# A five-place ring for streamed weight factors, paid for with one buffer less for factors on their way out

## The chip, the cores and the metric

The kernel runs on one core of a Trainium2 chip. A core has a matrix engine (PE; its weight loads are shown apart as PEld), a vector engine (DVE), a scalar engine (ACT), a general-purpose engine (POOL), a queue processor that here issues nearly all transfers (SP), and 16 DMA engines. The metric is the device time of one execution in microseconds (us), as the median over runs. Before the change it is 1222.57 us over 3 runs (1222.3 to 1227.66).

## The reference

Linear attention with softmax-like features feeds a gated two-layer product. The sizes are 8 batches, 8 heads, 576 tokens of 64 dimensions, 128 features; then 4608 tokens, 512 model columns and 1536 hidden columns, all in 32 bits.

```python
def phi(x):
    proj = einsum('bhsd,df->bhsf', x, w_phi)
    proj = proj - max(abs(proj), axis=-1, keepdims=True)
    return concatenate([exp(proj), exp(-proj)], axis=-1)
q_p, k_p = phi(q), phi(k)
kv = einsum('bhsf,bhsd->bhfd', k_p, v)
z = sum(k_p, axis=2)
attn = einsum('bhsf,bhfd->bhsd', q_p, kv) / (einsum('bhsf,bhf->bhs', q_p, z)[..., None] + 1e-06)
x = attn.transpose(0, 2, 1, 3).reshape(4608, 512)
out = (x @ w_a) * (x @ w_b) @ w_out
```

## The kernel before

Every matrix product of the second half is made of three products of split values: a 32-bit number is kept as a high part and a low part (a cast on ACT, then a subtraction on DVE; the helper `split`, L153 and L160), and PE multiplies high by high, high by low and low by high.

**First pass.** Hidden columns 0 to 767 (six slices of 128) are worked on while attention still runs, in 12 blocks of 384 tokens (`moe_block`). A block makes `pa` and `pb` for each slice (L616), multiplies the two (a copy on ACT, L620, and a product on DVE, L621), splits the result into `hh` and `hl`, and at its end makes four output accumulators `po` (L639), which are copied out (L651) to a DRAM tensor `part`. The output products of a block need `hh` and `hl` of all its slices. The last four blocks, numbers 8 to 11, run after attention has ended.

**Second pass.** Hidden columns 768 to 1535 are worked on in six blocks j = 0 to 5 of 768 tokens, with a scheme of seven products of half-size factors instead of eight (`winograd`). The weights are grouped in three quads q = 0, 1, 2, each with seven factors named w11, w12, s2, s1, s3, w22, s4. I write (q, k) for one of them. One product takes the factor of w_a and the factor of w_b, 12 matmuls in all (L729); the output products (L840) take factors of w_out.

**Where the factors live.** `load_factors` makes the factors during blocks 8 to 11: raw weights come in by DMA, ACT and DVE decode them, and each factor is split into a tile of 128 x 2 x 256 values (256 KB). Those of w_a and w_b leave for DRAM (L541, tensors `kept_...`); the first three pairs also stay in tiles `first0` to `first2`. The tile of a factor that leaves has tag `kept` with five buffers (L538): a sixth factor must wait until the store of the first has landed. ACT makes the cast, so it is ACT that waits.

The 21 factors of w_out all stay, two to a tile, in the places of w_a and w_b that the first pass has done with (`home(f, nm)`, 12 places). 21 is odd: the eleventh tile is half empty. One of the 12 places is left, and after the first pass its six places of w_out come free too: seven places of 512 KB. Four become the ring (`RING`, L55), three hold parts of the output that are read back.

**The ring.** A pair of factors is fetched (`fetch`, L565, 512 KB, called `back_...`) into a place of the ring when the product that used the place is done. `feed` is called behind each product of `winograd`, and it fetches the pair that the ring needs next in that place. So with four places the pair for product n is asked for when product n-4 has ended. All fetches, loads of x for the next block (L669), read-backs of `part` (L818) and stores of the output (L825) stand in one queue on SP, which issues them in order and stops at the first that may not go yet.

**What sets the order.** The kernel is written as nested generators, but the order of instructions on each engine is set by a scheduler that simulates the program when it is built (`schedule_with_timeline_sim=True`). In the second pass's block j = 0 the products are held to the written order (`in_turn`); in blocks 1 to 5 the scheduler may put a product ahead of others. It sees the buffers and their waits, so a change of a buffer's number moves instructions elsewhere.

Of the kernel before, what the change touches and what calls it, by code (L numbers as in the profile page):

```python
# [11 lines left out]
F32R = mybir.dt.float32r  # L12
# [6 lines left out]
P = 128  # L19
# [32 lines left out]

SLICES0 = 6
T1, T2 = 384, 768
RING, FIRST = 4, 3  # L55

FACTORS, AHEAD = ("w11", "w12", "s2", "s1", "s3", "w22", "s4"), 3.2
BLOCKS_LAST = 4
# [3 lines left out]
def tile_kernel(ctx, tc, qP, qD, km, kr, vm, vr, w_phi, w_two, eye, w_a, w_b, w_out, out):  # L62
# [14 lines left out]
    B, H, _, S = qD.shape  # L77
# [79 lines left out]
    def split(hi, lo, src, eng_hi, eng_lo):  # L157

        copy(eng_hi, hi, src)
        eng_lo.tensor_tensor(lo, src, hi, op=ALU.subtract)  # L160
# [294 lines left out]
    def decode(raw, u, stage):  # L455

        low, high = raw[:, :, 0], raw[:, :, 1]
        w = stage("w", [P, 2 * DM], F32, f"w_{u}")
        g, s = w[:, :DM], w[:, DM:]
        gb, sb = g.bitcast(U32), s.bitcast(U32)
        nc.scalar.activation(g, high.bitcast(F32), AF.Prelu, scale=2.0**-112, alpha=2.0**32)
        nc.vector.tensor_scalar(sb, gb, 3, None, op0=ALU.logical_shift_left)  # L470
        yield
        nc.vector.tensor_scalar(gb, sb, 0xFF800000, None, op0=ALU.bitwise_and)
        yield
        nc.vector.scalar_tensor_tensor(g, low, 2.0**-52, g, op0=ALU.mult, op1=ALU.mult)
        return s, g

    def load_raw(p, f, nm, stage):

        cols = (sum(NFS[:p]) + f) * P
        src = {"a": w_a, "b": w_b, "o": w_out}[nm]  # L480
        raw = stage("raw", [P, DM, 2], U32, f"raw_{p}_{f}_{nm}")
        if nm == "o":
            nc.sync.dma_start(raw.rearrange("p n w -> p (n w)"), src[cols : cols + P, :].bitcast(U32))
        else:
            nc.sync.dma_start(
                raw.rearrange("p (c n) w -> p c (n w)", c=NCC),
                src.bitcast(U32)[:, 2 * cols : 2 * (cols + P)].rearrange("(c p) n -> p c n", p=P),
            )
        return raw
# [14 lines left out]
    def load_factors(q, nm, stage, places, pool):  # L504

        w32 = stage("w32", [P, 2, DM], F32, f"w32_q{q}_{nm}")
        w = [w32[:, i] for i in range(2)]
        for i in range(2):
            u = f"q{q}_{nm}_{i}"
            s, g = yield from decode(load_raw(1, 2 * q + i, nm, stage), u, stage)  # L510
            nc.vector.tensor_tensor(w[i], s, g, op=ALU.add)
            yield
        n = DM // 2
        (w11, w12), (w21, w22) = ((t[:, :n], t[:, n:]) for t in w)
        if nm == "o":
            w12, w21 = w21, w12
        sums = stage("ws", [P, 4, n], F32, f"ws_q{q}_{nm}")
        s1, s2, s3, s4 = (sums[:, i] for i in range(4))
        nc.vector.tensor_tensor(s1, w21, w22, op=ALU.add)
        nc.vector.tensor_tensor(s3, w11, w21, op=ALU.subtract)  # L520
        nc.vector.tensor_tensor(s2, s1, w11, op=ALU.subtract)
        nc.vector.tensor_tensor(s4, w12, s2, op=ALU.subtract)
        factors = dict(w11=w11, w12=w12, s2=s2, s1=s1, s3=s3, w22=w22, s4=s4)
        yield
        for k, w32 in factors.items():
            key, i = two[q, nm, k]
            shape = [P, 2, 2, n]
            name = "_".join(map(str, key))
            if key not in begun:
                begun.add(key)  # L530
                if nm != "o":
                    kept[key] = dpool.tile(shape, F32, name=f"kept_{name}")
                if key in places:
                    weights[key] = places[key][0].tile(shape, F32R, tag=places[key][1], name=f"own_{name}")
            if key in places:
                t = weights[key][:, i]
            else:
                t = pool.tile([P, 2, n], F32R, tag="kept", bufs=5, name=f"wf_q{q}_{nm}_{k}")  # L538
            split(t[:, 0], t[:, 1], w32, nc.scalar, nc.vector)
            if nm != "o":  # L540
                nc.sync.dma_start(kept[key][:, i], t.bitcast(F32))  # L541
            if k in ("w12", "s1", "w22"):
                yield
        yield
# [13 lines left out]
    def stage_second(xin, pool):  # L558

        tags = {"raw": (pool, "raw"), "w": (pool, "w"), "w32": (xin, "x32"), "ws": (pool, "w")}  # L560
        return lambda kind, shape, dt, name: tags[kind][0].tile(shape, dt, tag=tags[kind][1], bufs=2, name=name)
# [355 lines left out]
    def run(work, steps=None):  # L917

        while work and steps != 0:
            if next(work[0], work) is work:  # L920
                work.popleft()
            elif steps is not None:
                steps -= 1
# [8 lines left out]
    def home(f, nm):  # L932
        return wpool, f"w_{f}_{nm}"

    kept, begun, feeds = {}, set(), []
# [28 lines left out]
    xin = ctx.enter_context(tc.tile_pool(name="xin", bufs=1))  # L964
    first_stack = ExitStack()
    first = first_stack.enter_context(tc.tile_pool(name="first", bufs=1))
    pairs = {(q, k): [(q, nm, k) for nm in "ab"] for q in range(nq) for k in FACTORS}
    outs = [(q, "o", k) for q in range(nq) for k in FACTORS]
# [7 lines left out]
    own = {key: (first, f"first{i}") for i, key in enumerate(order[:FIRST])}  # L976
    xs = [{} for _ in range(NCC // 2)]
    with ExitStack() as c:
        pool = c.enter_context(tc.tile_pool(name="stage", bufs=1))
        stage = stage_second(xin, pool)  # L980
        ahead = itertools.chain(
            *(load_factors(q, nm, stage, own, pool) for q in range(nq) for nm in "ab"),
            factors_of_x(0, xin, xs),
        )
        last = work.pop()
        due = 0.0
        while work:
            run(work, 1)
            due += AHEAD
            while due >= 1:  # L990
                next(ahead, None)
                due -= 1
        for _ in ahead:
            pass
        next(last)
        outs = deque(pair for pair in pairs if pair[0] == "o")
        places = deque()
        for f in range(NFS[0]):
            next(last)
            for nm in "ab":  # L1000
                if outs:
                    own[outs.popleft()] = home(f, nm)
                else:
                    places.append(home(f, nm))
            if f % 2:
                for _ in load_factors(f // 2, "o", stage, own, pool):
                    pass
# [15 lines left out]
    while len(ring) < RING:  # L1023
        ring.append(places.popleft())
        key = order.popleft()
# [64 lines left out]
```

## Time and profile before

| what | value |
|---|---|
| median of 3 runs | 1222.57 us |
| the profiled execution | 1223.55 us |
| its span, first to last instruction | 1221.8 us |
| PE busy | 1188.0 us (97%) |
| DVE busy | 969.6 us (79%) |
| ACT busy | 779.1 us (64%) |
| granted TensorE clock, mean | 0.997 |

The profiled execution is 0.98 us above the median, and 1.75 us of it lie outside the span. Its profile cuts the span by engine, by group of instructions and by the chain of waits that ended last. The first pass's lone blocks take 691 to 809 us of the span, the second pass 809 to 1222 us, about 68 us for each of its six blocks.

### The profile page before, as it was taken

The numbers are of one execution on the slowest core, as the hardware profiler recorded it, in microseconds if no ns is written. First come the engines' busy times: TensorE is split into PE (matmuls) and PEld (weight loads), VectorE is DVE, ScalarE is ACT, GpSimd is POOL, SyncE is SP. The second block draws the span as 40 slices with busy tenths as digits, with TensorE's granted clock in tenths as the row PEclk, the third lists the DMA queues.
The fourth block names the chain that finished last, engine by engine and source line by source line (L and its number), as shares of the span: only waits on it lengthen the run. The fifth ranks groups of instructions, "written<-read, shape, count | busy, mean of one in ns | idle before, by whom it ended". The sixth has DMA issues, their size and how long they took to land.

```text
span 1221.8 us, 20189 instructions
## 1 busy us (share of the span) xinstructions
PE 1188.0 (97%) x7086; PEld 1132.8 (93%) x7086; DVE 969.6 (79%) x1733; ACT 779.1 (64%) x1656; POOL 153.2 (13%) x68
## 2 busy tenths in 40 slices
PE   8889999999999999999999999999999999999998
PEld 5567789999999999999999999999999999999997
DVE  6866888988998989898888378978768695868665
ACT  5777778878878878888788445644435352535332
POOL 2322222211222121121122000000000000000000
PEclk9999999999999999999999999999999999999999
DMA  8766764554455454545342578758586777768582
GB/s 235 220 212 178 189 187 121 152 157 123 142 144 151 132 151 118 154 135 166 108 131 55 161 242 292 255 163 315 173 272 203 233 237 225 245 202 288 171 252 82
DMA packets 146165, 225.13 MB, mean 184 GB/s; under 512 B 40912, under 2 KB 87760, under 8 KB 146064
## 3 DMA queue, kind: packets, MB, share of 16 engines
q1 hardware_dynamic: 145616, 223.58, 59.9%
q8 instruction: 56, 0.92, 0.3%
q14 instruction: 45, 0.37, 0.1%
q10 hardware_dynamic: 448, 0.26, 0.1%
HBM read 174.74 MB, written 49.05 MB: 183 GB/s over the span
## 4 chain that ended last, share of the span: by engine, by line
PE 77%; DMA 11%; DVE 7%; ACT 2%; issue 2%; SPq 1%; DVEq 0%; ACTq 0%
PE pa L616 11%; PE pb L616 11%; PE po L639 11%; PE po L840 9%; PE pa L729 9%; PE pb L729 8%; PE kvps L301 7%; PE pn L383 6%; PE pq L359 2%; DMA back_w<-kept_w 2%; PE pk L244 2%; DMA x<-xnorm 2%; DMA raw_a<-in_w_a 1%; DMA raw_o<-in_w_out 1%; DMA rec<-r 1%
## 5 line engine op out<-in xcount | busy, mean ns | idle before, releaser
L363 POOL PARTITION_ALL_REDUCE mb<-p x64 | 153.0, 2391 | 526.4 <-ACT p L360 416.8
L616 PE MATMUL pa<-xh,w_a 128*128 128x384 f32 x576 | 168.1, 344 | 3.9 <-ACT xh L153 2.2
L616 PE MATMUL pb<-xh,w_b 128*128 128x384 f32 x576 | 163.2, 341 | 0.0
L639 PE MATMUL po<-hh,w_o 128*128 128x384 f32 x576 | 154.4, 340 | 1.1 <-ACT o L651 0.7
L616 PEld LDWEIGHTS pa<-xh,w_a 128*128 128x128 f32 x576 | 106.0, 188 | 5.6 <-ACT xh L153 2.4
L639 PEld LDWEIGHTS po<-hh,w_o 128*128 128x128 f32 x576 | 104.7, 188 | 2.1 <-ACT o L651 1.0
L616 PEld LDWEIGHTS pb<-xh,w_b 128*128 128x128 f32 x576 | 105.5, 188 | 0.5
L616 PE MATMUL pa<-xl,w_a 128*128 128x384 f32 x288 | 98.4, 342 | 0.0
L639 PE MATMUL po<-hl,w_o 128*128 128x384 f32 x288 | 97.4, 340 | 0.6 <-DVE hl L160 0.6
L616 PE MATMUL pb<-xl,w_b 128*128 128x384 f32 x288 | 97.5, 338 | 0.0
L160 DVE TENSOR_TENSOR qel<-qe,qeh 128x1152 fp32r<-128x1152 f32 x46 | 62.3, 1354 | 31.2 <-ACT qeh L153 29.5
L840 PE MATMUL po<-hh_s,own_o 128*128 128x384 f32 x288 | 80.3, 336 | 0.6 <-DVE o L822 0.3
L165 DVE TENSOR_TENSOR qs<-q,qs 64x576 fp32r<-64x576 f32 x52 | 63.2, 1216 | 14.3 <-ACT qs L153 12.1
L384 ACT COPY xn<-pn 65x288 f32<-65x288 f32 x128 | 49.0, 394 | 17.0 <-PE pn L383 14.8
L840 PE MATMUL po<-hh_w,own_o 128*128 128x384 f32 x216 | 59.1, 334 | 0.0
L639 PEld LDWEIGHTS po<-hl,w_o 128*128 128x128 f32 x288 | 54.0, 188 | 1.2 <-DVE hl L160 1.2
L153 ACT CAST qeh<-qe 128x1152 fp32r<-128x1152 f32 x46 | 53.3, 1160 | 2.1 <-PE pn L383 2.0
L258 ACT ACTIVATE ke<-kd 128x512 f32<-128x512 f32 x64 | 40.8, 637 | 21.4 <-DVE kd L250 20.3
L616 PEld LDWEIGHTS pa<-xl,w_a 128*128 128x128 f32 x288 | 54.1, 188 | 0.3
L616 PEld LDWEIGHTS pb<-xl,w_b 128*128 128x128 f32 x288 | 54.1, 188 | 0.1
L367 ACT ACTIVATE qe<-p 128x576 f32<-128x576 f32 x64 | 44.5, 696 | 15.1 <-DVE qel L160 10.1
L840 PEld LDWEIGHTS po<-hh_s,own_o 128*128 128x128 f32 x288 | 52.6, 188 | 1.6 <-DVE o L822 0.6
(301 smaller groups left out, 3419.5 us busy)
## 6 DMA issues: line engine op xcount, KB each, us to landing
back_s<-kept_s SPq DMA_DIRECT2D x71, 512.0 KB
back_w<-kept_w SPq DMA_DIRECT2D x52, 512.0 KB
q<-in_qD SPq DMA_DIRECT2D x52, 288.0 KB
k<-in_km SPq DMA_DIRECT2D x55, 256.0 KB
xun<-xn SPq DMA_DIRECT2D x64, 144.0 KB
x<-xun SPq DMA_DIRECT2D x32, 288.0 KB
rb<-rec SPq DMA_DIRECT2D x32, 288.0 KB
xnorm<-x SPq DMA_DIRECT2D x32, 288.0 KB
```

What stands on the lines that cost most here:

```text
L153: eng.copy(dst, src)
L160: eng_lo.tensor_tensor(lo, src, hi, op=ALU.subtract)
L165: eng_lo.tensor_tensor(hi_lo[D:], src[D:], hi_lo[D:], op=ALU.subtract)
L301: nc.tensor.matmul(st["kv_ps", b, pr][:width, j], v_[:, j, :width], e_[:, j], start=(left == NFULL and j == 0 and n_ == 0), stop=(left == ...
L363: nc.gpsimd.partition_all_reduce(mb, p32, P, bass_isa.ReduceOp.absmax)
L367: nc.scalar.activation(e[:, 0], p32, AF.Exp)
L383: nc.tensor.matmul(pn[: D + 1, :HALF], kv_[:, 2 * j + s, :], e_[:, s, tok], **at)
L384: nc.scalar.copy(xn[: D + 1, tok], pn[: D + 1, :HALF])
L616: nc.tensor.matmul(acc, w[:, cc * P : (cc + 1) * P], x, start=(k == 0), stop=(k == 3 * NCC - 1))
L639: nc.tensor.matmul(accs[cc], w[:, cc * P : (cc + 1) * P], h, **at)
L729: in_turn(lambda: nc.tensor.matmul(acc[to][i], w_, x_, skip_group_check=True, **at), u.startswith("1_0"))
L840: in_turn(lambda: nc.tensor.matmul(acc[m, to], w_, h_, skip_group_check=True, **f), False)
```

## The change

- The ring has five places for four.
- When one pair of w_out is left (the single factor (2, s4)), it gets a tile of its own in the pool `xin`, and the place that it would have half filled is left for the ring. The shape of a tile follows the number of factors that share it.
- Tag `kept` has four buffers for five. A buffer is 128 x 2 x 256 values, as large as the new tile.

The whole diff:

```diff
-RING, FIRST = 4, 3
+RING, FIRST = 5, 3
...
             key, i = two[q, nm, k]
-            shape = [P, 2, 2, n]
+            shape = [P, len(pairs[key]), 2, n]
             name = "_".join(map(str, key))
...
             else:
-                t = pool.tile([P, 2, n], F32R, tag="kept", bufs=5, name=f"wf_q{q}_{nm}_{k}")
+                t = pool.tile([P, 2, n], F32R, tag="kept", bufs=4, name=f"wf_q{q}_{nm}_{k}")
             split(t[:, 0], t[:, 1], w32, nc.scalar, nc.vector)
...
             for nm in "ab":
+                if len(outs) == 1:
+                    own[outs.popleft()] = xin, "single"
                 if outs:
                     own[outs.popleft()] = home(f, nm)
                 else:
```

The scheduler answers with another order from block 10 of the first pass on. Two places matter below.

**PE, second pass, block j = 2.** One row of each product is shown, the first matmul of its w_a half; the number behind `back_` counts the fetched pairs, then come quad and factor. Before:

```order
L729 MATMUL pa0_1_2_2_12050<-xw11h_1_2_0_11477,back_51_2_w11_11948 128x384
...
L729 MATMUL pa0_1_2_1_11888<-xs3h_1_2_0_11660,back_50_1_s3_11934 128x384
...
L729 MATMUL pa1_1_2_2_12066<-xw12h_1_2_0_11509,back_52_2_w12_11994 128x384
...
L729 MATMUL pa0_1_2_1_11888<-xw22h_1_2_0_11664,back_53_1_w22_12010 128x384
...
L729 MATMUL pa0_1_2_2_12050<-xs2h_1_2_0_11641,back_55_2_s2_12064 128x384
...
L729 MATMUL pa2_1_2_1_11996<-xs4h_1_2_0_11733,back_54_1_s4_12035 128x384
...
L729 MATMUL pa2_1_2_2_12163<-xs1h_1_2_0_11645,back_56_2_s1_12080 128x384
```

The same stretch after the change:

```order
L729 MATMUL pa0_1_2_2_12052<-xw11h_1_2_0_11479,back_50_2_w11_11936 128x384
...
L729 MATMUL pa1_1_2_2_12068<-xw12h_1_2_0_11511,back_51_2_w12_11950 128x384
...
L729 MATMUL pa2_1_2_2_12165<-xs1h_1_2_0_11647,back_55_2_s1_12066 128x384
...
L729 MATMUL pa0_1_2_1_11890<-xw22h_1_2_0_11666,back_52_1_w22_11996 128x384
...
L729 MATMUL pa2_1_2_1_11998<-xs4h_1_2_0_11735,back_53_1_s4_12012 128x384
...
L729 MATMUL pa0_1_2_2_12052<-xs2h_1_2_0_11643,back_54_2_s2_12037 128x384
```

Product (1, s3), whose row is not shown in the second fence, now stands between (2, w12) and (2, s1). Before, (2, w11) stood ahead of (1, s3) and its written place is behind it; now (2, s1) stands ahead of three products that are written before it.

**SP, the same block.** `x32` are loads of x for the next block, with 576 and 192 columns. Before:

```order
L565 DMA back_51_2_w11_11948<-kept_2_w11_9366 128x1024
L669 DMA x32_1_3_0_11980<-xnorm4_94 128x2x576
L565 DMA back_52_2_w12_11994<-kept_2_w12_9371 128x1024
L565 DMA back_53_1_w22_12010<-kept_1_w22_9080 128x1024
L669 DMA x32_1_3_0_11980<-xnorm5_95 128x2x192
L565 DMA back_55_2_s2_12064<-kept_2_s2_9376 128x1024
```

After:

```order
L565 DMA back_50_2_w11_11936<-kept_2_w11_9366 128x1024
L565 DMA back_51_2_w12_11950<-kept_2_w12_9371 128x1024
L669 DMA x32_1_3_0_11982<-xnorm4_94 128x2x576
L565 DMA back_52_1_w22_11996<-kept_1_w22_9080 128x1024
L565 DMA back_53_1_s4_12012<-kept_1_s4_9085 128x1024
L669 DMA x32_1_3_0_11982<-xnorm5_95 128x2x192
L565 DMA back_55_2_s1_12066<-kept_2_s1_9381 128x1024
```

One more fetch stands ahead of each load of x, and (2, s1) is fetched ahead of (2, s2).

**ACT, first pass, block 10.** `wf_q1_b_s4` is the cast of factor (1, s4) of w_b; `h32_0_10_4` and `hh_0_10_4` belong to slice 4 of block 10. Before:

```order
L153 CAST wf_q1_b_s4_9241<-ws_q1_b_9173 128x256
L469 ACTIVATE w_q2_a_1_9289<-raw_1_5_a_9287 128x512
L620 COPY h32_0_10_4_9795<-pa_0_10_4_9769 128x384
L153 CAST hh_0_10_3_9757<-h32_0_10_3_9754 128x384
L153 CAST wf_q2_a_w11_9367<-w32_q2_a_9278 128x256
L153 CAST wf_q2_a_w12_9372<-w32_q2_a_9278 128x256
L153 CAST hh_0_10_4_9798<-h32_0_10_4_9795 128x384
```

After:

```order
L153 CAST hh_0_10_3_9757<-h32_0_10_3_9754 128x384
L153 CAST wf_q1_b_s4_9241<-ws_q1_b_9173 128x256
L620 COPY h32_0_10_4_9795<-pa_0_10_4_9769 128x384
L469 ACTIVATE w_q2_a_1_9289<-raw_1_5_a_9287 128x512
L153 CAST wf_q2_a_w11_9367<-w32_q2_a_9278 128x256
L153 CAST wf_q2_a_w12_9372<-w32_q2_a_9278 128x256
L153 CAST hh_0_10_4_9798<-h32_0_10_4_9795 128x384
```

The cast of slice 3 has moved ahead of factor (1, s4), and the copy of slice 4 still stands behind it.

## Rows read from the trace of the kernel before

**Rows 1.** The page of the profile: span, the busiest engine, and the chain that ended last, by engine (shares of the span).

```profile
span 1221.8 us, 20189 instructions
PE 1188.0 (97%) x7086; PEld 1132.8 (93%) x7086; DVE 969.6 (79%) x1733; ACT 779.1 (64%) x1656; POOL 153.2 (13%) x68
PE 77%; DMA 11%; DVE 7%; ACT 2%; issue 2%; SPq 1%; DVEq 0%; ACTq 0%
```

**Rows 2.** Stretches of the span (us from its start): length, then busy time and number of instructions of PE, PEld, DVE, ACT, POOL, then the granted clock, the DMA engines' busy share and GB/s. The third to the fifth are parts of the second pass's blocks 1 and 2.

```profile
200.00:700.00 500.00, 497.75 (x3309) 492.48 (x3307) 425.81 (x643) 409.60 (x842) 103.03 (x42) 1.00 0.47 135
700.00:809.00 109.00, 107.75 (x607) 106.85 (x606) 95.68 (x227) 60.64 (x143) 0.00 (x0) 1.00 0.74 250
893.00:917.00 24.00, 23.15 (x132) 22.55 (x131) 17.70 (x37) 10.11 (x23) 0.00 (x0) 1.00 0.88 295
917.00:961.00 44.00, 43.38 (x249) 42.74 (x248) 31.77 (x64) 18.32 (x41) 0.00 (x0) 1.00 0.63 199
961.00:985.00 24.00, 22.30 (x129) 22.01 (x128) 18.33 (x38) 9.85 (x22) 0.00 (x0) 1.00 0.89 295
```

**Rows 3.** What PE waited for from 840 us to the end: total us, times, longest.

```profile
PE pa L729 <- DMA back_w<-kept_w: 5.2, 4, 1.8
PE pa L729 <- ACT low L737: 0.9, 2, 0.5
...
PE pa L729 <- DMA back_s<-kept_s: 0.4, 1, 0.4
```

**Rows 4.** PE in order of time, matmuls that had to wait (start, length, then in brackets the idle time before them and what ended it).

```profile
924.21 0.44 PE L729 MATMUL pa<-xw22h,back_w 128*128 128x384 f32 x1 [0.46 <-ACT low L737]
969.86 0.41 PE L729 MATMUL pa<-xw11h,back_w 128*128 128x384 f32 x1 [1.70 <-DMA back_w<-kept_w]
1037.43 0.41 PE L729 MATMUL pa<-xw11h,back_w 128*128 128x384 f32 x1 [1.81 <-DMA back_w<-kept_w]
1128.31 0.44 PE L729 MATMUL pa<-xw22h,back_w 128*128 128x384 f32 x1 [0.46 <-ACT low L737]
1172.47 0.41 PE L729 MATMUL pa<-xw11h,back_w 128*128 128x384 f32 x1 [0.19 <-ACT top L737]
```

**Rows 5.** The chain that ended last, in order of time (start, length, what): the fetches and a load of x that stand on the chain, and two runs of 12 matmuls, as many as one product has.

```profile
895.91 4.85 DMA back_w<-kept_w
964.03 5.69 DMA back_w<-kept_w
1031.49 5.81 DMA back_w<-kept_w
1041.86 6.51 DMA back_s<-kept_s
1099.73 4.85 DMA back_w<-kept_w
1111.75 7.15 DMA x<-xnorm
1174.79 2.08 PE pa L729 x12
1176.87 2.08 PE pb L729 x12
```

**Rows 6.** SP in order of time in block 2 and, last, in block 5 (start, length, what it issues, and how many together).

```profile
964.03 0.32 SPq L565 DMA_DIRECT2D back_w<-kept_w  x1
964.44 0.39 SPq L669 DMA_DIRECT2D x<-xnorm  x1
966.11 2.40 SPq L565 DMA_DIRECT2D back_w<-kept_w  x2
...
1168.15 4.49 SPq L565 DMA_DIRECT2D back_w<-kept_w  x3
```

**Rows 7.** The chain that ended last, first pass, end of block 10.

```profile
752.05 4.54 DMA kept_s<-wf_q_b_s
...
756.95 0.42 ACT wf_q_a_w L153
...
757.73 0.55 DVE h L621
```

**Rows 8.** ACT in order of time in the same stretch.

```profile
751.32 0.41 ACT L153 CAST wf_q_b_s<-ws_q_b 128x256 fp32r<-128x256 f32 x1 [0.15 <-DMA kept_w<-wf_q_b_w]
753.52 0.68 ACT L469 ACTIVATE w_q_a<-raw_a 128x512 f32<-128x512 f32 x1 [1.79 <-DVE w_q_a L511]
754.10 0.46 ACT L620 COPY h<-pa 128x384 f32<-128x384 f32 x1
756.95 0.76 ACT L153 CAST wf_q_a_w<-w_q_a 128x256 fp32r<-128x256 f32 x2 [1.97 <-DMA kept_s<-wf_q_b_s]
758.31 0.51 ACT L153 CAST hh<-h 128x384 fp32r<-128x384 f32 x1 [0.60 <-DVE h L621]
```

**Rows 9.** DVE there, one step of the decoding of a weight, and PE there, two matmuls that had to wait.

```profile
754.70 0.43 DVE L472 TENSOR_SCALAR w_q_a<-w_q_a 128x512 uint32<-128x512 uint32 x1
...
758.88 0.44 PE L639 MATMUL po<-hh,w_o 128*128 128x384 f32 x1 [0.42 <-ACT hh L153]
759.73 0.44 PE L639 MATMUL po<-hl,w_o 128*128 128x384 f32 x1 [0.41 <-DVE hl L160]
```

## Prediction

> **What bounds the kernel now.** I read the page first: PE is busy for 97% of the span and carries 77% of the chain that ended last; DMA has 11% of it and DVE 7% [rows 1]. Then the stretches: the granted clock is 1.00 in all of them, so PE runs at the higher of its levels (2.4 GHz), and the change leaves the number of matmuls as it is. PE misses 0.85 us in 893 to 917 us and 1.70 us in 961 to 985 us, both in the last third of a block, and only 0.62 us in the 44 us between [rows 2]. So a gain can come only from gaps in PE, and these are few. The view of PE's waits over the second pass names them: 5.2 us in four waits, the longest 1.8 us, for fetched factors of kind w, 0.4 us once for one of kind s, and 0.9 us for `low`, a copy that ACT makes [rows 3]. 5.6 us is all that a deeper ring can win by itself.
>
> PE in order of time gives the place: 1.70 us at 969.86 and 1.81 us at 1037.43, each at the first matmul of (2, w11) [rows 4]. The other two share 5.2 - 1.70 - 1.81 = 1.7 us, 0.85 us each; one of them is the 0.85 us that PE misses in block 1 [rows 2]. The chain says why. A fetch for (2, w11) took 4.85, 5.69, 5.81 and 4.85 us in blocks 1 to 4 [rows 5]. PE needs it two products after it was asked for, and a product of 12 matmuls takes 2.08 us [rows 5], so 4.16 us. In block 2: 964.03 + 5.69 = 969.72, and PE starts 0.14 us later [rows 4, 5]. SP issues a load of x 0.4 us behind that fetch [rows 6], and the two share the DMA engines, which are 88 to 89% busy here against 63% between [rows 2]. Block 5 has no next block to load x for: the fetch is issued at 1168.15, and PE starts (2, w11) at 1172.47 after 0.19 us of waiting for `top`, a copy of ACT [rows 4, 6]. There the fetch took at most 4.3 us.
>
> **A, what the fifth place removes.** The fetch for a product goes out when the product five before it has ended. (2, w11) then has three products, 6.24 us, between issue and use, and (2, w12) as many. The longest of these fetches, 5.81 us, and the 0.14 us behind it make 5.95 us, so both are hidden. The wait for (1, s4), whose fetch took 6.51 us in block 3 [rows 5] and which is the 0.43 us of kind s [rows 3], has in its new place at least four products. A = -(0.85 + 1.70 + 1.81 + 0.85 + 0.43) = -5.64 us.
>
> **B, what takes its place.** The scheduler has used the room to draw another product forward: (2, s1) now stands ahead of (1, w22), (1, s4) and (2, s2). Its pair is number 55 in block 2, and 55 - 5 = 50 is (2, w11). Between the end of (2, w11) and the start of (2, s1) only (2, w12) and (1, s3) are left, again two products, 4.16 us. That is the slack which was too short for (2, w11). It is so in blocks 2, 3 and 5; in blocks 1 and 4 half of (1, w22) also stands between, which makes 4.16 + 1.04 = 5.20 us. The landing of this fetch is not in the trace, so I bound it by the five fetches of rows 5: 4.85 at the short end, 6.51 at the long one, 5.54 us on the mean. With 0.14 us behind the landing, the wait is 5.54 + 0.14 - 4.16 = 1.52 us in blocks 2 and 3 and 0.48 us in 1 and 4. Block 5 has no load of x: 4.3 + 0.14 - 4.16 gives at most 0.28 us, and I take 0.1. B = 2 x 1.52 + 2 x 0.48 + 0.1 = +4.1 us. At the short end 2 x 0.83 = +1.7; at the long end 2 x 2.49 + 2 x 1.45 + 0.28 = +8.2. I take the mean, because one more load of x, of 192 columns, stands on SP just ahead of this fetch, as one stood just behind the other. Behind the waiting matmul PE holds (1, w22) and (1, s4), whose factors are there, so the loss is not made up.
>
> The Trainium skill ("Perfetto Trace Analysis", section Identifying Performance Opportunities) says that the same gap repeating on the engine which should be saturated can mean too few buffers for the next tile. By it the cure is complete: the term would be A alone. That is the first rival below. The trace has the gap at one product, in the four blocks that load x; it agrees on the cause and does not decide whether the gap only moves.
>
> **C, the copy `low`.** PE waits 0.46 us for it at (2, w22) in two blocks [rows 4]. After the change (2, w22) stands right behind (2, s3) in four blocks. At worst all four wait, 4 x 0.46 - 0.9 = +0.9; at best nothing changes. I take +0.5.
>
> **D, four buffers for kept factors.** With five, the cast of w11 of w_a in quad 2 waits for the store of (1, s2) of w_b: 752.05 + 4.54 = 756.59 us, and ACT starts the cast at 756.95 after 1.97 us of waiting [rows 7, 8]. With four, it is the cast of (1, s4) of w_b, at 751.32 before, that needs this store. ACT now holds behind it the copy `h` of slice 4 (0.46), a step of decoding (0.68), two casts (0.76) and the cast of that slice's `hh` [rows 8]. After 756.59 + 0.36 = 756.95 the path to PE is: cast 0.41, copy 0.46, then the product `h` on DVE. DVE has in its own order, ahead of that product, steps of the decoding (0.43 us each [rows 9]) which need ACT's 0.68. With 0.68 and one of these the product starts at 756.95 + 0.41 + 0.46 + 0.68 + 0.43 = 758.93 and, at 0.55 us [rows 7], ends at 759.48. Before it ended at 757.73 + 0.55 = 758.28. So `hh` and `hl` of slice 4, for which the output products already wait 0.42 + 0.41 us [rows 9], come 1.2 us later; with a second step of DVE and its start behind ACT it is up to 2.0. I take +1.8 us. The low end is -0.83, if the order in which hh of slice 3 is now cast first lets PE find all of it ready. The high end is a store that lands as late as the longest transfer of rows 5, 7.15 - 4.54 = 2.6 us later: 1.8 + 2.6 = +4.4.
>
> The row has 4.54 us for the store of 256 KB. The Trainium skill ("DMA: Bandwidth & Descriptors", section Anatomy of one DMA — SWDGE (gpsimd) path) gives 2.0 us and the bytes at 436 GB/s, an estimate of 2.6 us, for transfers issued on another path. By that the buffer is free before the cast could want it, and D would be 0 or below. The trace disagrees, and its duration is used.
>
> The rest costs nothing. The new tile's own place adds no instruction: 21 factors are cast as before, and the place that it gives up was half empty. The additional first fetch of the ring has all of block 0, whose products keep the written order; with five places each of its pairs is asked for four products, 8.3 us, ahead of use, over the 6.51 us of the slowest fetch. From 200 to 700 us PE is busy for 497.75 of 500 us [rows 2], and that stretch casts no factor.
>
> **The sum.** -5.64 + 4.1 + 0.5 + 1.8 = +0.8 us on 1223.55, the profiled execution: 1224.3. That execution is 0.98 us above the median, so I forecast a median of 1223.3 us, no change. The bounds of the terms: at the low end -5.64 + 1.7 + 0 - 0.83 = -4.8, 1217.8; at the high end -5.64 + 8.2 + 0.9 + 4.4 = +7.9, 1230.4.
>
> **The rivals.** R1: the ring cures the wait and nothing follows. The fetch of (2, s1) lands within 4.16 us, as that of block 5 did within 4.3. Then A stands alone, and with block 10's 0.83 us gone too: 1222.57 - 5.64 to - 6.5, 1216.1 to 1216.9. For it: the 192-column load of x is small and issued about one product earlier. Against it: none of five fetches in blocks with x took under 4.85 us.
>
> R2, the slower side: the four buffers decide. In blocks 10 and 11 each batch of seven casts meets the round trip of a store, and ACT stands still with copies of `h` behind it, which PE waits for. At the high end of D, once in each of the two blocks, that is 8.8 us: -5.64 + 4.1 + 0.5 + 8.8 = +7.8, 1230.4. It decides from the point where the first pass gives back more than 7.2 us, since then the sum passes +6.1. For it: DMA is 74% busy from 700 to 809 us and moves 250 GB/s, against 135 before [rows 2]. Against it: PE there loses only 1.25 us in 109, and ACT is busy for 60.64 us of them, so that a stall of 2 us is caught up soon.
>
> R3: the change doesn't do what it says. Fetches stand in one queue on SP, and a fetch that could go one product earlier may be held by what stands ahead. Then the gaps at (2, w11) stay, and C is not touched; D alone gives 1222.57 + 1.8 = 1224.4. Against it: the order has the fetch one place further up, ahead of the load of x, with nothing between that waits longer.
>
> **How the numbers follow.** Forecast 0.63, R1 0.17, R2 0.12, R3 0.08. Half a per cent, 6.1 us, is about what a measurement of this kernel can tell from no change: 1216.5 and 1228.7. The forecast's own range, 1217.8 to 1230.4, lies almost wholly in between; R1's 1216.1 to 1216.9 lies on its lower edge. That gives faster 0.08, half of R1; slower 0.11, nearly all of R2; same 0.81. The range that I give, 1216.5 to 1229, leaves out that half of R1, R2, and nothing else of weight: under 0.2.
>
> **What would show it.** In the profile after: no wait of PE for a w factor in blocks 1 to 4 (A); waits for an s factor at the first matmul of (2, s1), about 1.5 us in blocks 2 and 3 and 0.5 us in 1 and 4, nearly none in 5 (B); up to four waits of 0.46 us for `low` (C); near 752 us a wait of ACT at the cast of (1, s4) that ends with a store's landing, and some 2.6 us of PE's waiting for `hh` and `hl` at the end of block 10 (D). If the fetch of (2, s1) lands in under 4.2 us, B is wrong and R1 has it; if PE waits over 7 us for `h`, `hh` or `hl` between 730 and 809 us, D is wrong and R2 has it; if (2, w11) still waits, A is.

## The result, and the profile after the change

The changed kernel takes 1232.74 us (median of 6 runs, 1227.89 to 1239.86) against 1222.57 us before: the ratio is 1.0081, with a 95% interval from 1.0056 to 1.0105. It is slower by 10 us, where 1223.3 us and no change were forecast, and lies above the range of 1216.5 to 1229.

The first lines of the changed kernel's page, as in [rows 1]; its profiled execution is the longest of the six.

```profile
span 1238.1 us, 20189 instructions
PE 1195.3 (97%) x7086; PEld 1139.5 (92%) x7086; DVE 971.6 (78%) x1733; ACT 778.9 (63%) x1656; POOL 151.4 (12%) x68
PE 68%; DMA 13%; DVE 10%; ACT 6%; issue 2%; SPq 1%; DVEq 0%; ACTq 0%
```

PE does the same 7086 matmuls and is busy 7.3 us longer, and ACT's share of the chain has gone from 2% to 6%. PE's waits from 840 us to the end, the view of [rows 3]:

```profile
PE pa L729 <- ACT low L737: 6.9, 5, 2.9
PE pa L729 <- DMA back_s<-kept_s: 3.2, 2, 1.7
PE po L840 <- DVE hl_s L748: 0.9, 1, 0.9
PE po L840 <- ACT u L828: 0.7, 2, 0.4
PE pa L729 <- ACT top L737: 0.6, 2, 0.4
```

The 5.2 us for w factors are gone. In their place stand 3.2 us for s factors, which were forecast, and 6.9 us for `low`, a copy on ACT that cost 0.9 us before. PE in order of time gives the places (start, length, in brackets the idle time before and what ended it):

```profile
767.49 0.69 PE L639 MATMUL po<-hh,w_o 128*128 128x384 f32 x1 [3.51 <-ACT hh L153]
...
920.04 0.57 PE L729 MATMUL pa<-xw22h,back_w 128*128 128x384 f32 x1 [2.61 <-ACT low L737]
...
938.59 0.44 PE L729 MATMUL pa<-xw22h,back_w 128*128 128x384 f32 x1 [0.46 <-ACT low L737]
990.24 0.41 PE L729 MATMUL pa<-xs1h,back_s 128*128 128x384 f32 x1 [1.42 <-DMA back_s<-kept_s]
...
1058.54 0.41 PE L729 MATMUL pa<-xs1h,back_s 128*128 128x384 f32 x1 [1.74 <-DMA back_s<-kept_s]
...
1128.02 0.44 PE L729 MATMUL pa<-xw22h,back_w 128*128 128x384 f32 x1 [2.95 <-ACT low L737]
```

The waits at 920.04 and 1128.02 are at (1, w22) in blocks 1 and 4. ACT in order of time shows what the copy `low` stood behind, and what held `hh` in block 10:

```profile
766.62 0.40 ACT L153 CAST wf_q_a_w<-w_q_a 128x256 fp32r<-128x256 f32 x1 [4.07 <-DMA kept_s<-wf_q_b_s]
766.93 0.51 ACT L153 CAST hh<-h 128x384 fp32r<-128x384 f32 x1
...
918.68 0.51 ACT L153 CAST xw11h<-x 128x384 fp32r<-128x384 f32 x1 [4.90 <-DMA x<-xnorm]
919.10 0.51 ACT L153 CAST xw12h<-x 128x384 fp32r<-128x384 f32 x1
919.52 0.47 ACT L737 COPY low<-pa 128x384 f32<-128x384 f32 x1
919.89 0.48 ACT L737 COPY low<-pb 128x384 f32<-128x384 f32 x1
```

In block 1 ACT stands still for 4.90 us at a cast of x for the next block. The last matmul of (1, s3) began at 916.92, 2.6 us before the first copy, but the copies of its sums stand behind two such casts, and (1, w22) adds to the same sums and may not start before they are copied. The kernel before had one of the two copies ahead of the first cast; its ACT in block 1:

```profile
904.32 0.48 ACT L737 COPY low<-pa 128x384 f32<-128x384 f32 x1 [0.56 <-PE pa L729]
907.50 0.52 ACT L153 CAST xw11h<-x 128x384 fp32r<-128x384 f32 x1 [2.70 <-DMA x<-xnorm]
907.92 0.47 ACT L737 COPY low<-pb 128x384 f32<-128x384 f32 x1
```

That only blocks 1 and 4 have this wait follows from the code around L669. It loads the 768 columns of the next x in two pieces, and for blocks 2 and 5 the first piece has 192 columns: a cast of the first 384 columns needs both. (In block 2 the copies stand behind the casts too, and the casts find their x there.) In the changed kernel's block 1 SP issued the second piece 4.1 us behind the first, with two fetches between them:

```profile
907.47 0.39 SPq L669 DMA_DIRECT2D x<-xnorm  x1
909.14 0.32 SPq L565 DMA_DIRECT2D back_w<-kept_w  x1
911.22 0.32 SPq L565 DMA_DIRECT2D back_s<-kept_s  x1
911.59 0.43 SPq L669 DMA_DIRECT2D x<-xnorm  x1
```

The chain that ended last has this load of x and, from block 10, the store that the cast at 766.62 waited for (start, length, what):

```profile
759.44 7.10 DMA kept_s<-wf_q_b_s
...
911.59 7.02 DMA x<-xnorm
```

The store that a buffer waited for took 7.10 us, against 4.54 us in [rows 7]; it is another factor's store of the same size, that of (1, s3) of w_b, the fourth kept factor ahead of the waiting cast. The last piece is the clock. Stretches of the changed kernel, with the columns of [rows 2]; the granted clock is the third number from the end:

```profile
700.00:809.00 109.00, 105.18 (x581) 104.24 (x580) 87.51 (x204) 55.40 (x131) 0.00 (x0) 0.97 0.75 240
764.00:768.00 4.00, 0.51 (x1) 0.29 (x1) 1.40 (x4) 1.38 (x4) 0.00 (x0) 0.82 0.83 266
768.00:772.00 4.00, 4.00 (x13) 3.92 (x13) 4.00 (x11) 2.59 (x7) 0.00 (x0) 0.50 0.54 162
772.00:776.00 4.00, 4.00 (x20) 4.00 (x20) 4.00 (x11) 2.21 (x6) 0.00 (x0) 0.82 0.63 232
776.00:780.00 4.00, 4.00 (x25) 4.00 (x24) 3.06 (x8) 1.77 (x5) 0.00 (x0) 1.00 0.96 275
...
918.00:924.00 6.00, 3.96 (x14) 3.96 (x15) 5.29 (x11) 2.60 (x6) 0.00 (x0) 0.72 0.87 290
...
1125.00:1131.00 6.00, 3.05 (x11) 2.98 (x11) 4.32 (x10) 2.57 (x6) 0.00 (x0) 0.78 0.98 384
```

Behind the wait of 3.51 us PE is "busy" for all of 768 to 776 us, but at 0.50 (1.2 GHz) and then 0.82 it makes 13 and 20 matmuls in 4 us, where 25 are usual. That is 17 matmuls, or 17 x 0.16 = 2.7 us, on top of the wait. Behind the 2.61 us, in 918 to 924 us, the clock was 0.72, and behind the 2.95 us, in 1125 to 1131 us, 0.78: there the starts of 10 to 12 matmuls lie 0.32 us apart in place of 0.17, some 1.6 us lost each time. This makes 5.9 of the 7.3 us by which the busy time grew with no work added.

Three marks cut each execution, read from PE in order of time: a wait of 0.31 us for `xn` that every profile has near 698 us, the first matmul of the second pass, and the end of the span. Before the first mark the order of instructions on each engine is the same in all kernels of this study (one memory clear on DVE aside), and that mark still lies anywhere from 693.7 to 702.3 us: that is the spread of executions. Behind it the lengths are:

| kernel (its profiled execution) | places, kept buffers | tail of the first pass | second pass |
|---|---|---|---|
| before | 4, 5 | 112.5 | 412.6 |
| changed | 5, 4 | 117.7 | 418.2 |

The tail is 5.2 us longer and the second pass 5.6 us; with 5.5 us of spread ahead of the first mark they are the 16.3 us of this span's difference, and without it 10.8 us, near the 10.2 us between the medians.

### The profile page after: what moved, and what is told of

The parts are those of the page before. It is cut to its first block, busy times and chain, and to the rows that moved or that the text cites. A ratio compares the mean times of both kernels' runs of the same rounds, so it can differ in the third digit from the quotient of the medians.

```text
span 1238.1 us, 20189 instructions
## 1 busy us (share of the span) xinstructions
PE 1195.3 (97%) x7086; PEld 1139.5 (92%) x7086; DVE 971.6 (78%) x1733; ACT 778.9 (63%) x1656; POOL 151.4 (12%) x68
## 4 chain that ended last, share of the span: by engine, by line
PE 68%; DMA 13%; DVE 10%; ACT 6%; issue 2%; SPq 1%; DVEq 0%; ACTq 0%
PE pa L729 10%; PE po L840 9%; PE pb L729 9%; PE pb L616 8%; PE pa L616 8%; PE po L639 8%; PE kvps L301 6%; PE pn L383 6%; DMA x<-xnorm 3%; PE pq L359 2%; DMA raw_a<-in_w_a 1%; DMA rec<-r 1%; PE pk L244 1%; DVE qs L165 1%; DMA back_s<-kept_s 1%
## 5 line engine op out<-in xcount | busy, mean ns | idle before, releaser
L840 PE MATMUL po<-hh_s,own_o 128*128 128x384 f32 x288 | 80.9, 336 | 1.1 <-ACT u L828 0.7
L840 PE MATMUL po<-hh_w,own_o 128*128 128x384 f32 x216 | 59.0, 334 | 0.0
L840 PEld LDWEIGHTS po<-hh_s,own_o 128*128 128x128 f32 x288 | 52.7, 188 | 2.4 <-ACT u L828 1.3
L153 ACT CAST hh<-h 128x384 fp32r<-128x384 f32 x72 | 37.2, 516 | 26.2 <-DVE h L621 26.0
```

What stands on the lines that cost most here:

```text
L153: eng.copy(dst, src)
L840: in_turn(lambda: nc.tensor.matmul(acc[m, to], w_, h_, skip_group_check=True, **f), False)
```

## Experiments

Theory 1: three separate waits add up, each with the lower clock behind it: the cast that waits for a store in block 10, the copies `low` behind casts of x in blocks 1 and 4, and the fetch of (2, s1). Theory 2 is R2 of the prediction: the four kept buffers decide alone. Theory 3: the second pass decides alone. All ratios are against the kernel before on the same chip, in brackets the 95% interval; tail and second pass are lengths in us between the marks, in the profiled execution of each.

| run | places, kept | order added | median us | before there | ratio | tail | second pass |
|---|---|---|---|---|---|---|---|
| r4_k4 | 4, 4 | none | 1228.50 | 1222.12 | 1.0072 [1.0044, 1.0101] | 116.0 | 414.1 |
| r4_k3 | 4, 3 | none | 1227.62 | 1222.12 | 1.0055 [1.0029, 1.0081] | 119.6 | 409.8 |
| r5_k5 | 5, 5 | none | 1229.54 | 1222.12 | 1.0068 [1.0041, 1.0095] | 116.7 | 419.3 |
| r5_low | 5, 4 | `low` first on ACT | 1230.59 | 1222.12 | 1.0077 [1.0052, 1.0101] | 112.5 | 416.2 |
| after_again | 5, 4 | none | 1236.57 | 1223.07 | 1.0093 [1.0060, 1.0126] | 118.2 | 421.1 |
| r5_k5_low | 5, 5 | `low` first on ACT | 1232.11 | 1223.07 | 1.0066 [1.0044, 1.0087] | 117.1 | 413.4 |
| r4_turn | 4, 5 | all products | 1233.37 | 1223.07 | 1.0083 [1.0060, 1.0107] | 113.5 | 418.9 |
| r5_k5_turn | 5, 5 | all products | 1236.83 | 1223.07 | 1.0109 [1.0090, 1.0129] | 115.9 | 420.8 |
| r4_chain | 4, 5 | four products | 1218.26 | 1221.67 | 0.9964 [0.9944, 0.9985] | 112.9 | 405.9 |
| r5_chain | 5, 4 | four products | 1221.04 | 1221.67 | 0.9996 [0.9979, 1.0014] | 115.4 | 406.9 |
| r5_k5_chain | 5, 5 | four products | 1220.03 | 1221.67 | 0.9990 [0.9975, 1.0006] | 115.1 | 405.9 |
| r4_k4_chain | 4, 4 | four products | 1220.15 | 1220.44 | 0.9989 [0.9969, 1.0010] | 117.1 | 407.8 |

**One part alone: r4_k4.**

```diff
-                t = pool.tile([P, 2, n], F32R, tag="kept", bufs=5, name=f"wf_q{q}_{nm}_{k}")
+                t = pool.tile([P, 2, n], F32R, tag="kept", bufs=4, name=f"wf_q{q}_{nm}_{k}")
```

> The kernel before with one number changed: four buffers for kept factors for five; the ring keeps four places. Theory 1 (three separate waits add up): the changed kernel lost in block 10 of the first pass 3.51 us of waiting for hh in place of 0.83, and behind it the granted clock was 0.50 for some 4 us and 0.82 for 4 more, some 2.7 us of work; so about half of the loss of 10.2 us is from this buffer. Expected: 1226 to 1229 us, PE waits about 3.5 us for hh near 760 us, the clock falls behind it, and the second pass is as before with its 5.2 us for w factors. Theory 2 (the first pass alone decides, rival R2 of the prediction): the full loss, 1231 to 1234. Theory 3 (the second pass alone decides): 1222 to 1224.

1228.5 us, in theory 1's range. PE waited 2.80 us in block 10, and the clock fell behind it: over 740 to 780 us it was 0.96.

```profile
762.78 0.62 PE L639 MATMUL po<-hh,w_o 128*128 128x384 f32 x1 [2.80 <-ACT hh L153]
```

Theory 3 falls, and theory 2 has not its full loss. The profiled execution is 6.4 us longer than that of before, as the medians are: 3.6 us of it lie in the tail, 1.5 in the second pass and 1.4 ahead of the first mark, inside the spread. One thing that was expected did not come: the second pass waited 2.7 us for w factors, in two waits, and not 5.2. It is longer all the same, since the clock was 0.72 for 6 us behind two of its waits, 1.93 us at 820.50 and 1.89 us at 977.74. The stretch behind the first, and the next:

```profile
821.00:827.00 6.00, 6.00 (x27) 6.00 (x26) 1.86 (x5) 1.50 (x4) 0.00 (x0) 0.72 0.00 1
827.00:833.00 6.00, 6.00 (x37) 6.00 (x36) 2.95 (x6) 2.33 (x5) 0.00 (x0) 1.00 0.75 199
```

**A stronger dose: r4_k3**, the same line with `bufs=3`.

> The kernel before with three buffers for kept factors for five; ring of four. A dose of the suspected cost: each cast must wait for the store three factors back, whose round trip was 4.54 us. If a store's landing is what holds ACT, then PE waits longer than with four buffers and at more places between 730 and 809 us, each wait with a lower clock behind it: 1231 to 1242. If the one wait in block 10 was an accident of the order there, the time is that of four buffers, 1223 to 1229.

1227.6 us, no more than with four buffers, and in the range that was given for an accident of the order. The tail is the longest of all, with 3.81 us of waiting for `hh` at the same place, but the second pass of the profiled execution was short. The dose is not seen in the time. The one new wait between block 10 and the second pass is 2.54 us just ahead of the latter; so one or two places in the order are exposed, and not every cast.

**The other part alone: r5_k5.** Every fifth factor goes through the tile of the single one:

```diff
-                t = pool.tile([P, 2, n], F32R, tag="kept", bufs=4, name=f"wf_q{q}_{nm}_{k}")
+                spun[0] = (spun[0] + 1) % 5
+                place = (pool, "kept", 4) if spun[0] else (xin, "single", 1)
+                t = place[0].tile([P, 2, n], F32R, tag=place[1], bufs=place[2], name=f"wf_q{q}_{nm}_{k}")
...
```

(Not shown: the counter `spun` starts at 0.)

> The changed kernel with five buffers for kept factors again: every fifth factor on its way out goes through the tile of the single odd factor of w_out, which is not written until all factors of w_a and w_b are made. Five places in the ring. Theory 1: block 10 is as before, and the second pass keeps its waits of 2.6 and 2.9 us for low in blocks 1 and 4 and of about 1.5 us for the pair of (2, s1) in blocks 2 and 3, with the clock lower behind the long ones: 1225 to 1229. Theory 2: 1217 to 1223. Theory 3: 1231 to 1234.

1229.5 us, a little over theory 1's range. The second pass is as long as that of the changed kernel, with the same waits, so the second pass loses with five kept buffers too.

```profile
PE pa L731 <- ACT low L739: 7.5, 5, 3.4
PE pa L731 <- DMA back_s<-kept_s: 2.6, 3, 1.4
```

But the tail did not come back: PE waits 1.19 us for `hh` in block 10, 1.32 us for `hl` in block 11 and 2.16 us ahead of the second pass, the last two at new places. The scheduler answers to this arrangement with another order in block 11, so it is no clean return to five buffers. The two parts alone cost 6.4 and 7.4 us, more together than the 10.2 us of both at once. So these two runs show that each part costs; how the 10 us divide between them is read from the changed kernel's profile and not shown by them.

**The copies `low` first: r5_low.** The casts of x for w11 and w12 are put behind `low` of (1, s3) on ACT:

```diff
-        evict(low, 0)
+        ins = evict(low, 0)
+        if q == 1:
+            lows.append(ins)
...
-                factor(c, k, x[c + i][:, :n])
+                with tc.issue_after(lows[-1].ins) if lows else nullcontext():
+                    factor(c, k, x[c + i][:, :n])
...
```

(Not shown: `lows` starts as an empty list, and `evict` returns the second of its copies.)

> The changed kernel with one order added on ACT: the casts of x for the next block (xw11h, xw12h) stand behind the two copies low of (1, s3) of the present block. Four kept buffers. Theory 1: in blocks 1 and 4 PE waited 2.61 and 2.95 us at (1, w22) since the copies low stood behind casts that waited 4.90 us for a load of x. With the order added these two waits go to under 0.5 us each, and so does the fall of the clock behind them (0.72 over 6 us): 5 to 9 us less than the changed kernel, 1224 to 1228. The waits for (2, s1) and block 10 stay. Rival: the copies are late for another reason (PSUM or the load of x itself holds PE next): the waits move to another line, and the time stays at 1231 to 1234.

The waits for `low` went as theory 1 said; the time, 1230.6 us, lies between the two ranges and is not clear of the changed kernel's. Of the 5.5 us of waiting that went, 3.0 came back as waits for the pair of (2, s1) in blocks 1 and 4 (1.51 and 1.47 us), which had been hidden behind the longer wait:

```profile
PE pa L730 <- DMA back_s<-kept_s: 6.8, 5, 2.1
PE pa L730 <- ACT low L738: 1.4, 3, 0.5
```

Block 10 cost nothing in this execution, the fastest of its six: PE waited 0.38 us there and the tail is that of before. Yet in the tail the order of PE, ACT, DVE and SP is that of the changed kernel, as it is in after_again and r5_chain (both below). With this one order the tail took 112.5 us here and 117.7, 118.2 and 115.4 us in those three; with the order of five buffers it took 112.5 to 113.5 us (before, r4_chain, r4_turn). The store that the cast waits for took 5.38 us here and 5.08 us in r5_chain:

```profile
752.45 5.38 DMA kept_s<-wf_q_b_s
...
755.68 5.08 DMA kept_s<-wf_q_b_s
```

In r5_chain PE waited 1.95 us for `hh` behind the shorter of the two. So with four buffers the tail varies by 5.7 us from execution to execution, and the length of that store alone does not settle it; what else does is open.

**The changed kernel once more: after_again.**

> The changed kernel once more, beside the variants, for a second profile of it. Its first profile was the longest of its six runs (1239.9 us against a median of 1232.7). Theory 1: 1230 to 1234; the waits in the second pass come back (2.6 to 3 us for low in blocks 1 and 4, 1 to 2 us for the pair of (2, s1) in blocks 2 and 3), while the wait in block 10 and the fall of the clock behind it may differ, since a store's landing varies: with four kept buffers it was 3.51 us in one profile and 0.38 us in another. The 5.5 us that the first profile lost before 702 us, where the order of both kernels is the same, do not come back. Rival: those 5.5 us belong to the change and come back.

1236.6 us, longer still and over theory 1's range. The waits of the second pass came back in place and size (6.2 us for `low`, 3.1 us for s factors), and block 10's with 4.30 us. Ahead of the first mark 3.0 us came back and not 5.5, inside the spread of the others.

**r5_k5_low**, the last two edits together.

> Five places, five kept buffers by way of the tile of the single factor, and on ACT the casts of x behind the copies low of (1, s3). The drawn-ahead product (2, s1) stays. Theory 1: the waits for low of 3.42 and 2.74 us and the lower clock behind them go (6 to 8 us), waits of 1 to 2 us for the pair of (2, s1) stay in four blocks and now show in blocks 1 and 4 too: 1223 to 1227. Rival (low was not what cost): 1228 to 1231.

```profile
PE pa L732 <- DMA back_s<-kept_s: 5.9, 5, 1.9
PE pa L732 <- ACT low L740: 1.4, 3, 0.5
```

The second pass of the profile is 5.9 us shorter than r5_k5's, but at 1232.1 us the median is over both ranges and its ratio, 1.0066, is r5_k5's (1.0068): inconclusive on the time. Theory 1 as stated is too simple, since what is taken from one wait is given to the next: (2, s1) still stands too near behind (2, w11).

**All products in the written order: r4_turn and r5_k5_turn.**

```diff
-                        in_turn(lambda: nc.tensor.matmul(acc[to][i], w_, x_, skip_group_check=True, **at), u.startswith("1_0"))
+                        in_turn(lambda: nc.tensor.matmul(acc[to][i], w_, x_, skip_group_check=True, **at), u.startswith("1_"))
```

> The kernel before, four places and five kept buffers, with the matmuls of the second pass's winograd products held to the written order in all blocks and not in block 0 alone. Then no product is drawn ahead: each fetch has three products, 6.24 us, between issue and use. Theory 1 (the waits for fetches are made by products drawn ahead of their turn, not by the number of places): the 5.2 us for w factors go to under 2, and 1 to 3 us of waits for copies (top, low) come in where the scheduler could fill before: 1217 to 1222. Rival (places are what is short): the waits for fetches stay near 5 us at another product, since a fetch beside loads of x takes up to 6.5 us, and copies come on top: 1223 to 1228.

> Five places, five kept buffers by way of the tile of the single factor, and the written order in all blocks. Each fetch has four products, 8.3 us, over the longest fetch of 6.5 us, and the copies low stand ahead of the casts of x on ACT. Theory 1: no wait for fetches at all, none of the waits of 2.7 to 3.4 us for low, so the second pass is 4 to 10 us shorter than that of five places without the order: 1218 to 1224. Rival (the fifth place itself costs, by more transfers in flight beside the loads of x): 1226 to 1231, with new waits for x in the second pass.

Both missed on the time and hit on the fetches. With four places as with five, not one wait for a fetch is left. What came instead is at the end of a block; r4_turn:

```profile
PE po L840 <- ACT hh_s L745: 6.1, 5, 1.2
PE po L840 <- ACT u L828: 1.6, 6, 0.3
```

The output products need `hh_s`, which ACT and DVE have yet to make. The view counts waits over 0.15 us alone, and by it r4_turn waits hardly longer than the kernel before (9.4 us against 8.8). Counted from the start of one matmul to the start of the next, over the usual 0.17 us, the output products (L840) lose 16.9 us in r4_turn's second pass and 2.6 us in that of before. Before, the scheduler filled this time with the next block's first products: in block 1 (0, w11) of block 2 starts at 930.56, among the output products, and in r4_turn at 951.94, behind them. So four places suffice for the fetches, and the order must leave that end of the block free.

**Four products in order: r4_chain and r5_chain.** From this a new theory: products of quad 2 that are drawn ahead make the waits, and the number of places matters little. In blocks 1 to 5 four products alone are tied:

```diff
+HOLD = {(2, "w11"): (1, "s3"), (2, "w12"): (2, "w11"), (2, "s2"): (1, "s4"), (2, "s1"): (2, "s2")}
...
-                        in_turn(lambda: nc.tensor.matmul(acc[to][i], w_, x_, skip_group_check=True, **at), u.startswith("1_0"))
+                        mm = lambda: nc.tensor.matmul(acc[to][i], w_, x_, skip_group_check=True, **at)
+                        with tc.issue_after(ends[HOLD[q, k]].ins) if (q, k) in HOLD and not u.startswith("1_0") else nullcontext():
+                            in_turn(mm, u.startswith("1_0"))
+            ends[q, k] = issued[0]
```

(Not shown: `ends` starts as an empty dictionary.)

> The kernel before, four places and five kept buffers, with an order for four products alone: in blocks 1 to 5, (2, w11) stands behind (1, s3), (2, w12) behind (2, w11), (2, s2) behind (1, s4), (2, s1) behind (2, s2). All else stays free, so that, unlike where every product was held to the written order, the next block's products can still fill the stage of the output products. Each fetch has three products, 6.24 us. Theory 1 (a product drawn ahead, not the number of places, made the waits): the second pass loses its 5.2 us for w factors and the 0.9 us for low, the first pass is that of before: 1215 to 1220. Rival (three products are too few beside loads of x, whose fetches took up to 6.5 us): waits of under 1 us at (2, w11) and (1, s4) stay and the time is 1220 to 1224. Rival 2 (any order given to PE costs what the full order did): 1228 to 1234.

> The changed kernel (five places, four kept buffers) with the same order for four products. On ACT the copies low then stand ahead of the casts of x in all blocks; each fetch has four products, 8.3 us. Theory 1: no wait for low over 0.5 us and none for fetched factors in the second pass, which is as short as with four places and this order; what stays is the first pass with its wait in block 10 and the clock behind it, 3 to 6 us over before: 1219 to 1226, 8 us or more under the changed kernel. Rival (the fifth place costs by itself): 1228 or more.

Both times came out in theory 1's ranges. PE's waits from 840 us on in r4_chain, and then in r5_chain:

```profile
PE pa L730 <- ACT top L741: 1.0, 5, 0.2
PE po L844 <- ACT u L832: 0.6, 2, 0.3
PE pa L730 <- DMA back_w<-kept_w: 0.4, 1, 0.4
PE pa L730 <- DMA back_s<-kept_s: 0.2, 1, 0.2
```

```profile
PE po L844 <- ACT u L832: 1.6, 4, 0.6
PE pa L730 <- ACT top L741: 1.2, 6, 0.2
```

The second pass falls from 418.2 and 421.1 us to 406.9 us with five places, and from 412.6 to 405.9 us with four. This order also puts the copies `low` ahead of the casts of x on ACT, with no word said to ACT. The changed kernel sheds all of its 10 us by it. r4_chain, with neither the fifth place nor the lost buffer, has the lowest time of all: 0.9964 of the kernel before, with an interval that lies under 1.

**The other corners: r5_k5_chain and r4_k4_chain**, the same order on r5_k5 and on r4_k4.

> The same with five kept buffers by way of the tile of the single factor. Second pass as in the run with four kept buffers. In the first pass this arrangement showed waits of some 1.2 us for hh in block 10, 1.4 us for hl in block 11 and 2.2 us ahead of the second pass in each of its three profiles, 3.4 to 4.6 us in all against before. Theory 1: 1218 to 1224, and within 3 us of the run with four kept buffers. Rival (four kept buffers are the larger part of the loss): 4 us or more under that run.

> Four places, the order for four products, and four kept buffers: the fourth corner of places by buffers under one and the same order in the second pass. Four places with five buffers lay 3.4 us under the kernel before, five places with four buffers 0.6 us under it. Theory: the first pass pays for the fourth buffer, some 3 us of waiting for hh in block 10 and of lower clock, and the fifth place earns nothing once the order is given; so 2 to 5 us over four places with five buffers, that is between 1.5 us under and 1.5 us over the kernel before (1220 to 1223). Rival (the fifth place does earn, and hid a larger cost of the buffer): 2 us or more over the kernel before.

Both times, 1220.0 and 1220.2 us, lie in the ranges expected. Under one order the second pass takes 405.9 to 407.8 us in all four corners, so the fifth place earns nothing that can be seen there: r4_chain still has 0.6 us of waits for fetches, and r4_k4_chain, with four places too, has none. Four kept buffers with four places lie at 0.9989 where five lie at 0.9964, some 3 us apart, as expected, though the intervals overlap; so do those of r4_chain and r5_k5_chain (0.9990). The tail of r4_k4_chain has the wait again, 2.75 us, with the granted clock 0.91 over 740 to 780 us.

```profile
740.00:780.00 40.00, 37.24 (x196) 36.62 (x194) 34.11 (x81) 22.43 (x54) 0.00 (x0) 0.91 0.78 262
```

## Why the prediction was wrong, point by point

**A held.** Neither profile of the changed kernel has the wait at (2, w11) or the one for (1, s4). -5.64 us was right, and R3 falls.

**B held in place and size** in blocks 2 and 3: 1.42 and 1.74 us against 1.52 each. In blocks 1 and 4, where 0.48 us were forecast, nothing was seen, but only as PE came there late from the longer wait; r5_low, without it, has 1.51 us (at 909.86) and 1.47 us (at 1116.99). 3.2 us in all against 4.1. R1 falls.

**C is the step that failed.** "At worst all four wait, 4 x 0.46 - 0.9 = +0.9" counted only (2, w22) behind (2, s3). That part came to three waits, 3 x 0.46 - 0.9 = +0.5, just what was taken. But the copy `low` was priced by its own length, with ACT free to make it, and the wait for it at (1, w22) was put at nothing. The large waits came at (1, w22), where the copies stand on ACT behind casts that wait for a load of x: 2.61 and 2.95 us in one profile, 2.50 and 2.33 in the other. Measured, the group is 6.9 and 6.2 us, +6.0 and +5.3 us against +0.5. The orders of SP ahead of the prediction showed one more fetch ahead of each load of x; what waits for that load was not followed to ACT, and ACT's order in blocks 1 and 4 has no part in the prediction.

**D was right in kind and undersized.** The wait in block 10, 0.83 us for `hh` and `hl` before, grew to 3.51 us, by 2.7 us, and in the second profile to 4.30 us, by 3.5 us: in the range up to 4.4 and over the 1.8 us taken. It was also another cast: that of (1, s4) waited only 0.19 us, and the second of the two w casts behind it waited 4.07 us, for a store that took 7.10 us.

**A term was missing: the clock.** The sum counted idle time alone. Behind the longer waits the granted clock fell: 2.7 us were lost so in block 10 and some 1.6 us each in blocks 1 and 4, 5.9 us in all. With them the terms as measured add up to -5.6 + 3.2 + 6.0 + 2.7 + 5.9 = +12.2 us, 1.4 more than the 10.8 us of the two lengths; that rest is not placed. R2 gave nearly the right time, 1230.4 us, by the wrong way: its condition, over 7.2 us in the first pass, is not met by tails that are 5.2 and 5.7 us longer, and half of the loss is in the second pass.

The deeper error: the prediction took the drawn-ahead product as given and repriced its one wait. The runs with four tied products show that the draw makes the second pass's waits for fetches and for `low`, before the change as after it, and that the order of ACT changes with it. The loss in the first pass is apart from this, and comes with the fourth buffer.

## What to carry to other kernels

A deeper buffer gives a scheduler room, and here it spent the room on pulling another instruction forward; the same gap then stood one step further on. Read the order of every engine that feeds the bottleneck, and for each small copy ask which transfer the instruction ahead of it waits for. Where a few instructions should not be drawn ahead, tie those few: here four tied products were worth more than a fifth place of 512 KB, and tying all of them made the kernel 10 us longer than before.

## What the runs showed of the hardware

A gap of a few microseconds in PE can cost more than its length. The clock fell to 0.50 behind 3.51 us in the changed kernel; 2.11 us in r5_low left 0.79 over the 6 us around it:

```profile
1044.00:1050.00 6.00, 3.89 (x16) 3.67 (x15) 4.93 (x11) 2.84 (x6) 0.00 (x0) 0.79 0.97 327
```

It did not follow every such gap: 2.22 us in r5_low at 815.77 left the clock at 1.00 over that block, as did 2.54 us in r4_k3 at 817.95, while 1.93 us in r4_k4 at 820.50, the same place as r5_low's, left 0.72 over 6 us, with 27 matmuls in them and 37 in the next 6. So equal waits do not cost equal time from run to run.

A 256 KB store of a factor in block 10 took 4.54 us before and 7.10 us in the changed kernel, another factor's; the latter's took from 5.08 us (r5_chain) to 7.10 us in executions with one and the same order. During the 7.10 us the DMA engines' busy share in stretches of 4 us lay between 0.58 and 0.98. The Trainium skill ("DMA: Bandwidth & Descriptors", section Anatomy of one DMA — SWDGE (gpsimd) path) would give an estimate of 2.6 us, for transfers issued on another path; none of the stores here comes near it.
